# Two transformer layers with dilated window attention and a SiLU feed-forward: the layout of two DRAM scratches, the release of second-layer weight loads, and the planner's landing times

## The chip, the core and the metric

The kernel runs on one core of one Trainium2 chip. Its engines are TensorE (PE in the profile, with weight loads as PEld), VectorE (DVE), ScalarE (ACT), GpSimd (POOL) and SyncE (SP). SP computes nothing here: it issues DMA loads, stores and DMA transposes. The metric is device microseconds of one execution. Before the change the median of three runs is 2185.98 us (2184.86 to 2187.14).

## The reference

One sequence of 2,048 tokens of width 576 goes through attention, feed-forward, attention, feed-forward, each with its own layer norm in front and a residual sum behind. Both layers use the same weights.

```python
H = 32; Dh = D // H          # 18
W, dil = 8, 2
idx = pos[:, None] - off[None, :]          # off = arange(W) * dil
mask = idx >= 0
logits = jnp.einsum("bhsd,bhswd->bhsw", q, kg) * scale
attn = _softmax(jnp.where(mask[None, None, :, :], logits, -1e9), axis=-1)
o = jnp.einsum("bhsw,bhswd->bhsd", attn, vg)          # then @ wo
...
h = _silu(jnp.einsum("bsd,df->bsf", x, w1))           # 576 -> 4608
out = jnp.einsum("bsf,fd->bsd", h, w2)                # 4608 -> 576
...
x = x + _A_ref(_layernorm(x, axis=-1), A_wqkv, A_wo)
x = x + _B_ref(_layernorm(x, axis=-1), B_w1, B_w2)    # both lines twice
```

A token attends to itself and to seven earlier tokens, two positions apart.

## The kernel before

**Stages.** The 2,048 tokens are cut into four chunks of 512 tokens (TB = 4 x 128): two halves of the sequence, and in each the even and the odd positions, so that a window of dilation 2 becomes eight neighbouring rows. Two layers times four chunks give eight stages s = 0 to 7. A stage has a front (load x, attention in four head groups u of 144 columns, projection with wo, layer norm) and a feed-forward. PE works in float16; a float32 value is split in a high and a low half, and a product takes three partial products.

**Feed-forward.** Stages 0 and 1 use plain tiles: 36 column blocks f of w1 (first product, line 1183) and of w2 (second product, line 1202). Stages 2 to 7 use pairs (`ffn_pairs`): two column blocks form a pair q, and each 2x2 block product is made of seven products P1 to P7 instead of eight, with sums of weights ("weight forms", seven 128x640 float16 tiles per pair) against sums of tokens ("token forms"). The seven products of a pair are line 1087, in the order P5, P1, P3, P6, P2, P7, P4. The 18 pairs of a stage are cut into groups of 5, 4, 5 and 4. When a group's hidden tiles stand, `second` (line 1141) multiplies them with the w2 tiles: for each of four token tiles j, and each pair, 12 matmuls.

**Scratches in DRAM.** Split weights go through DRAM: `w1s`, `w2s` (one tensor per block), and `wfs[q]` for the weight forms, which `prepare` makes on DVE, ACT and POOL between stages 0 and 2 and stores from GpSimd (line 1012). `wfs[q]` is 128 rows of 7 x 640 values, so that one form is 128 pieces of 1,280 bytes, 8,960 bytes apart. Keys and values that are computed ahead in stage 0 go to `kd[par][u]`, one row of 288 float32 values (1,152 bytes) per token, stored by SP (line 686); the attention of stages 1 to 3 fetches, for each partition, 11 neighbouring rows as one run of 12,672 bytes (line 713; stage 1 from SP, stages 2 and 3 from GpSimd).

**Buffers.** There are 12 slots for weight forms (`wf`) and 11 for w2 tiles (`w2`). A load takes the next slot, and SP waits until PE has finished with what was there.

**What sets the order.** The instructions aren't issued where they are written. Each `op(engine, duration, function, reads, writes, prio, ...)` goes into a `Plan`. `Plan.order()` plays the whole program through with the given durations, and on each engine starts the ready operation with the lowest `prio` whose slots are free. A transfer is taken to run at `DMA_RATE`, to begin `DMA_IN` after its issue and to be landed `DMA_OUT` after its last byte. The sequence found in this way is then each engine's program. On the chip each engine works through its list in order: an instruction whose semaphore isn't there holds up all that stand behind it on the same engine. So a number in the plan changes no work, but it can change the order on all five engines.

**Names used below.** `load_wf` (line 1015) loads one weight form (160 KB), `load_w2` (856) one w2 tile (288 KB), `load_wq` one qkv weight (1,080 KB), `load_w1` one w1 block. `transposed` (459) turns layer-normed or attention tiles by DMA transpose, `forms` (1062) the token forms. In the trace a `wf` slot bears the name of its memory, `w`; the token forms lie in `xb`; `yh` and `yo` are the tiles that are turned.

## Time and profile before

| | |
|---|---|
| median of 3 runs | 2185.98 us |
| profiled execution, its own time | 2186.47 us |
| its span on the core | 2184.3 us |
| PE busy | 2119.9 us (97%) |
| DVE busy | 1605.7 us (74%) |
| ACT busy | 954.5 us (44%) |
| POOL busy | 364.3 us (17%) |
| granted clock of TensorE, mean | 0.994 |

Between the span and the execution's own time lie 2.2 us. Read the profile like this: first the busy shares, which tell the engine that is short of idle time; then the waits of that engine, each with what ended it; then the time line around the longest of these waits on the engine that waits and on the queue that it waits for. A busy share is a mean over stages with different limits, so what one wait is worth is read where it stands.

### The profile page before, as it was taken

Reading aid. Unit: us, or ns where it says so; the run is one execution under the profiler, and the core shown is the slowest. Engines: PE = TensorE matmul, PEld = TensorE weight load, DVE = VectorE, ACT = ScalarE, POOL = GpSimd, SP = SyncE. Lnnn points to the kernel's source line nnn. Section 1 sums busy time; section 2 is a strip of 40 time slices with the busy share of each in tenths; the row PEclk is TensorE's granted clock in tenths of the full one; section 3 lists DMA queues with packets and bytes.
Section 4 is the critical chain, followed back from the end, with each engine's and each line's share of the span. In section 5 each row is a group of like instructions: output and inputs, shape, how many; then the busy total and the mean of one; then the engine's idle time right before and its main releaser. Section 6 shows DMA issues by size and latency. Waiting matters only on the chain.

```text
span 2184.3 us, 41276 instructions
## 1 busy us (share of the span) xinstructions
PE 2119.9 (97%) x16198; PEld 1578.8 (72%) x16198; DVE 1605.7 (74%) x2539; ACT 954.5 (44%) x1795; POOL 364.3 (17%) x585
## 2 busy tenths in 40 slices
PE   6999999999999899999999999999999999999999
PEld 3546566656666678876788768887787867888887
DVE  7999998999896897548974599646995569852222
ACT  7545687644344453443324434243433424343232
POOL 2133556234333140001100010000000000000000
PEclk9999999999999999999999999999999999999999
DMA  6476777587879785876539666496655855565443
GB/s 178 149 208 240 244 260 250 176 277 268 194 183 314 229 273 176 197 232 187 165 104 254 164 205 179 111 263 156 203 161 148 237 155 149 160 182 176 140 149 108
DMA packets 334234, 426.19 MB, mean 195 GB/s; under 512 B 145608, under 2 KB 262708, under 8 KB 330072
## 3 DMA queue, kind: packets, MB, share of 16 engines
q1 hardware_dynamic: 292464, 289.10, 47.3%
q0 software_dynamic: 38304, 129.28, 18.3%
q10 hardware_dynamic: 3272, 5.19, 0.9%
q8 instruction: 126, 2.06, 0.4%
q14 instruction: 68, 0.56, 0.1%
HBM read 307.32 MB, written 67.68 MB: 172 GB/s over the span
## 4 chain that ended last, share of the span: by engine, by line
PE 81%; DVE 8%; DMA 7%; ACT 2%; issue 1%; POOL 1%; SPq 0%; ACTq 0%; DVEq 0%
PE acc L1141 25%; PE misc L1087 11%; PE z L1087 11%; PE z L670 8%; PE acc L1202 8%; PE z L1183 7%; PE misc L670 5%; PE acc L841 4%; DMA w<-wfs 3%; DVE lg L773 1%; DVE pr L802 1%; DVE pr L769 1%; DVE pr L809 1%; DMA w<-w2s 1%; DMA wq<-in_B_w_dram 1%
## 5 line engine op out<-in xcount | busy, mean ns | idle before, releaser
L1141 PE MATMUL acc<-w,h 128*128 128x288 f16 x5184 | 653.7, 286 | 2.2 <-DVE h L1120 1.6
L1141 PEld LDWEIGHTS <-h 128*128 128x128 f16 x5184 | 506.5, 98 | 130.4 <-DVE h L1120 1.9
L1087 PEld LDWEIGHTS <-w 128*128 128x128 f16 x5292 | 518.9, 98 | 97.3 <-DMA w<-wfs 21.4
L1087 PE MATMUL z<-xb,w 128*128 128x256 f16 x2653 | 339.2, 275 | 14.0 <-DMA w<-wfs 9.9
L1087 PE MATMUL misc<-xb,w 128*128 128x256 f16 x2639 | 333.9, 273 | 10.4 <-DMA w<-wfs 8.6
L848 DVE SCALAR_TENSOR_TENSOR x<-acc,d,x 128x576 f32<-128x576 f32 x135 | 109.5, 812 | 179.1 <-PE acc L1141 171.2
L670 PEld LDWEIGHTS <-xa 128*128 128x128 f16 x1344 | 132.1, 99 | 116.7 <-issue 9.3
L1202 PE MATMUL acc<-w,h 128*128 128x288 f16 x1728 | 214.6, 286 | 0.0
L1202 PEld LDWEIGHTS <-h 128*128 128x128 f16 x1728 | 168.9, 98 | 43.9
L769 DVE TENSOR_TENSOR pr<-qt,kvs 128x2304 f32<-128x2304 f32 x64 | 163.4, 2553 | 34.6 <-DMA kvs<-kvs 24.7
L802 DVE TENSOR_TENSOR pr<-kvs,pe 128x1152 f32<-128x1152 f32 x128 | 169.9, 1352 | 1.1
L773 DVE TENSOR_REDUCE lg<-pr 128x128 f32<-128x2304 f32 x64 | 163.0, 2547 | 1.1
L809 DVE TENSOR_TENSOR pr<-pr 128x1152 f32<-128x1152 f32 (+1 forms) x128 | 135.2, 1056 | 3.4
L1183 PE MATMUL z<-xb,w 128*128 128x512 f16 x588 | 130.8, 383 | 6.0 <-ACT w L918 2.4
L1120 DVE SCALAR_TENSOR_TENSOR h<-wq,sh,h 128x1024 f16<-128x1024 f32 x60 | 76.9, 1281 | 72.6 <-ACT h L1117 72.6
L670 PE MATMUL z<-wq,xa 128*128 128x432 f16 x588 | 114.1, 350 | 4.2 <-ACT w L683 4.2
L841 PE MATMUL acc<-wo,yo 128*128 128x288 f16 x896 | 115.9, 289 | 2.3 <-DMA yo<-yh 2.2
L670 PE MATMUL misc<-wq,xa 128*128 128x432 f16 x588 | 113.1, 349 | 0.8 <-ACT qt L740 0.8
L1183 PEld LDWEIGHTS <-w 128*128 128x128 f16 x588 | 57.5, 98 | 76.6 <-DVE w L920 2.9
L841 PEld LDWEIGHTS <-yo 128*128 128x128 f16 x896 | 88.1, 99 | 27.1 <-DMA yo<-yh 2.7
L750 POOL DMA_DIRECT2D kvs<-kvs x64 | 33.8, 535 | 374.8 <-ACT qt L740 348.1
L1183 PE MATMUL z<-xb,wq 128*128 128x512 f16 x420 | 93.2, 379 | 0.7 <-ACT hs L1185 0.7
(227 smaller groups left out, 2495.5 us busy)
## 6 DMA issues: line engine op xcount, KB each, us to landing
w<-wfs SPq DMA_DIRECT2D x756, 160.0 KB
w<-w2s SPq DMA_DIRECT2D x252, 288.0 KB
wq<-wqs SPq DMA_DIRECT2D x17, 1080.0 KB
kvs<-kd POOLq DMA_DIRECT2D x8, 1584.0 KB, 8.6
w<-w1s SPq DMA_DIRECT2D x36, 320.0 KB
wfs<-xa POOLq DMA_DIRECT2D x18, 640.0 KB, 4.9
w2s<-w POOLq DMA_DIRECT2D x36, 288.0 KB, 4.1
w1s<-wq POOLq DMA_DIRECT2D x30, 320.0 KB, 4.1
```

The lines of the kernel that those rows point to most:

```text
L670: nc.tensor.matmul(T(m)[:, :3 * UC], a, b, start=n == 0, stop=n == len(pl) - 1)
L769: nc.vector.tensor_tensor(T(pr), T(qt)[:, j:j + 2, None, :].to_broadcast([P, 2, W, UC]), win(T(kv), j, 2), op=ALU.mult)
L773: nc.vector.tensor_reduce(T(lg)[:, j:j + 2].rearrange("p a w h -> p (a w h)"), T(pr).rearrange("p a w (h d) -> p (a w h) d", d=DH), axis=A ...
L802: nc.vector.tensor_tensor(T(pr)[:, a].rearrange("p w (h d) -> p w h d", d=DH), v, T(pe)[:, j + a, :, :, None].to_broadcast([P, W, UH, DH]) ...
L809: nc.vector.tensor_tensor(t[:, :, 0:h, :], t[:, :, 0:h, :], t[:, :, h:2 * h, :], op=ALU.add)
L841: nc.tensor.matmul(T(acc)[:, h, 0:288], a, b[:, h * 288:(h + 1) * 288], start=n == 0, stop=n == len(pl) - 1)
L848: nc.vector.scalar_tensor_tensor(t, T(acc)[:, :, 0:288], d, t, op0=ALU.mult, op1=ALU.add)
L1087: nc.tensor.matmul(t, w[:, u, :], v[:, r, :], start=first and m == 0, stop=m == 6, skip_group_check=True)
L1120: op("DVE", 1.2, lambda hq=hq, h=h, sc=sc: nc.vector.scalar_tensor_tensor(T(h)[:, 1].rearrange("p f t -> p (f t)"), T(hq).rearrange("p r t ...
L1141: nc.tensor.matmul(T(acc)[:, h, 0:288], T(hb[t])[:, a, f, j * P:(j + 1) * P], T(wbs[t][f])[:, w, h * 288:(h + 1) * 288], start=t == 0 and ...
L1183: nc.tensor.matmul(T(z), v, u, start=m == 0, stop=m == len(pl) - 1)
L1202: nc.tensor.matmul(T(acc)[:, h, 0:288], T(hb[q])[:, a, j * P:(j + 1) * P], T(wbs[q][0])[:, w, h * 288:(h + 1) * 288], start=q == 0 and m = ...
```

## The change

Five edits:

1. **Key scratch pitch.** A row of `kd` becomes 2 x 144 + 16 = 304 values (1,216 bytes), of which 288 are used. A fetch now reads 11 pieces of 1,152 bytes per partition instead of one run of 12,672 bytes.
2. **Weight forms in blocks.** `wfs[q]` becomes seven blocks of 128 x 640: one form is a contiguous 160 KB. A store from GpSimd writes 4 or 3 pieces of 1,280 bytes per partition instead of one run of 5,120 or 3,840 bytes.
3. **Second weights later.** In a group, the two w2 loads of the third, fourth and fifth pair get one more condition: the product P5 of the pair two before must have been done.
4. **More time in the plan.** An op has a new field `extra`, which is added to the landing time: 3.0 for the DMA transposes of `transposed` at positive priority, 2.0 for those of `forms`, 1.0 for the loads of weight forms. No instruction is added for it.
5. **`product` returns its op**, so that 3 can name it.

```diff
-    def op(self, eng, dur, fn, reads=(), writes=(), prio=0.0, nbytes=0, table=None, after=(), lanes=1):
+    def op(self, eng, dur, fn, reads=(), writes=(), prio=0.0, nbytes=0, table=None, after=(), lanes=1, extra=0.0):
         o = Op()
+        o.extra = extra
...
-                        o.end = clock + self.DMA_OUT
+                        o.end = clock + self.DMA_OUT + o.extra
...
-    wfs = [tc.dram_tile([P, 7 * KB], F16, name=f"wfs{q}") for q in range(NP)]
+    wfs = [tc.dram_tile([7, P, KB], F16, name=f"wfs{q}") for q in range(NP)]
...
+    KP = 2 * UC + 16
...
-    kd = [[tc.dram_tile([W - 1 + 2 * TB, 2 * UC], F32, name=f"kd{p}{u}") for u in range(NU)] for p in range(2)]
+    kd = [[tc.dram_tile([W - 1 + 2 * TB, KP], F32, name=f"kd{p}{u}") for u in range(NU)] for p in range(2)]
...
         return op("SP", 1.34, lambda: nc.sync.dma_start_transpose(dst(), fl(T(src))), [(src, 0), (src, 1)], [(key, j)], prio,
-                  nbytes=P * 9 * P * 4)
+                  nbytes=P * 9 * P * 4, extra=3.0 if prio > 0 else 0.0)
...
-                nc.sync.dma_start(rows(kd[par][u], W - 1 + blk * TB + j, [[NJ * 2 * UC, P], [1, 2 * UC]]),
+                nc.sync.dma_start(rows(kd[par][u], W - 1 + blk * TB + j, [[NJ * KP, P], [1, 2 * UC]]),
                                   stage(g)[:, UC:])
...
-                    q.dma_start(T(kv).rearrange("p a b c -> p (a b c)"),
-                                rows(kd[par][u], row, [[NJ * 2 * UC, P], [1, NI * 2 * UC]]))
+                    q.dma_start(T(kv).rearrange("p a b c -> p a (b c)"),
+                                rows(kd[par][u], row, [[NJ * KP, P], [KP, NI], [1, 2 * UC]]))
...
-    def load_w2(f, prio, kind="w2"):
+    def load_w2(f, prio, kind="w2", after=()):
         w = Buf(kind)
-        op("SP", 0.38, lambda: nc.sync.dma_start(fl(T(w)), w2s[f]), [("w2s", f)], [w], prio, nbytes=P * 4 * D)
+        op("SP", 0.38, lambda: nc.sync.dma_start(fl(T(w)), w2s[f]), [("w2s", f)], [w], prio, nbytes=P * 4 * D, after=after)
...
-                wfs[q][:, r0 * KB:r1 * KB], T(g).rearrange("p i a b -> p (i a b)")), [(g, 0)], [("wfs", q, r0 // 4)], prio, nbytes=P * n * KB * 2)
+                wfs[q][r0:r1].rearrange("i p c -> p i c"), T(g).rearrange("p i a b -> p i (a b)")), [(g, 0)], [("wfs", q, r0 // 4)], prio, nbytes=P * n * KB * 2)
...
-        op("SP", 0.38, lambda: nc.sync.dma_start(fl(T(w)), wfs[q][:, i * KB:(i + 1) * KB]), [("wfs", q, i // 4)], [w], prio, nbytes=P * KB * 2)
+        op("SP", 0.38, lambda: nc.sync.dma_start(fl(T(w)), wfs[q][i]), [("wfs", q, i // 4)], [w], prio, nbytes=P * KB * 2, extra=1.0)
...
                 op("SP", 1.26, lambda f=f, a=a, x=x: nc.sync.dma_start_transpose(T(x)[:, :, a * P:(a + 1) * P], T(f)[:, a]),
-                   [(f, a, 0), (f, a, 1)], [(x, a)], prio, nbytes=P * KB * 4)
+                   [(f, a, 0), (f, a, 1)], [(x, a)], prio, nbytes=P * KB * 4, extra=2.0)
...
-                w2b = [load_w2(2 * q + f, pd) for f in range(2)]
+                w2b = [load_w2(2 * q + f, pd, after=begun[-2:-1] if q > q0 + 1 else ()) for f in range(2)]
...
-                    op("PE", 0.763, mm, [wf[k], (xf[k], 0), (xf[k], 1)], [z], pp)
+                    return op("PE", 0.763, mm, [wf[k], (xf[k], 0), (xf[k], 1)], [z], pp)
...
-                product("P5", c, True, False)
+                begun.append(product("P5", c, True, False))
```

The line numbers of the changed kernel are two or three higher (858 becomes 861, 1017 becomes 1020, 1062 becomes 1065, 1245 becomes 1248). Up to the beginning of stage 1's second half PE's order stays as it is. Behind it the order changes on all engines. Three places of SP's queue:

**SP, the loads for the first group of stage 2**, the first stage in pairs. `wfs1` to `wfs4` are the weight forms of pairs 1 to 4, `w2s2` to `w2s10` the w2 blocks of pairs 1 to 5, two blocks to a pair, `x5` is an x tile of stage 3. Before:

```order
L1245 DMA x5_79<-in_A_x_dram 128x576
L858 DMA w2_93<-w2s2_162 128x1152
L858 DMA w2_93<-w2s3_163 128x1152
L858 DMA w2_93<-w2s4_164 128x1152
L858 DMA w2_93<-w2s5_165 128x1152
L858 DMA w2_93<-w2s6_166 128x1152
L858 DMA w2_93<-w2s7_167 128x1152
L858 DMA w2_93<-w2s8_168 128x1152
L858 DMA w2_93<-w2s9_169 128x1152
L858 DMA w2_93<-w2s10_170 128x1152
L1017 DMA w1_70<-wfs1_197 128x640 x2
L1017 DMA w1_70<-wfs2_198 128x640 x7
```

Now, at the same place:

```order
L861 DMA w2_93<-w2s4_164 128x1152
L861 DMA w2_93<-w2s5_165 128x1152
L1020 DMA w1_70<-wfs1_197 128x640
L1248 DMA x5_79<-in_A_x_dram 128x576
L1020 DMA w1_70<-wfs2_198 128x640 x7
L1020 DMA w1_70<-wfs3_199 128x640 x7
L861 DMA w2_93<-w2s6_166 128x1152
L861 DMA w2_93<-w2s7_167 128x1152
L1020 DMA w1_70<-wfs4_200 128x640 x7
L861 DMA w2_93<-w2s8_168 128x1152
```

Nine w2 loads stood in one block ahead of the rest of the weight forms. Now four stand ahead, among the last forms of pair 1, and the others behind the forms of pairs 3 and 4. In stages 3 to 7 most blocks of this kind are spread in the same way; in stage 2's later groups they still stand together.

**SP, the end of stage 1's loads**, where the token forms of stage 2 are turned; `w1s33` to `w1s35` are the last w1 blocks of stage 1. Before:

```order
L858 DMA w2_93<-w2s35_195 128x1152
L1062 DMA_TRANSPOSE xb_67<-yo_73 128x5x128 x2
L853 DMA w1_70<-w1s33_157 128x1280
L858 DMA w2_93<-w2s0_160 128x1152
L853 DMA w1_70<-w1s34_158 128x1280
L858 DMA w2_93<-w2s1_161 128x1152
L853 DMA w1_70<-w1s35_159 128x1280
```

Now:

```order
L861 DMA w2_93<-w2s35_195 128x1152
L1065 DMA_TRANSPOSE xb_67<-yh_91 128x5x128
L861 DMA w2_93<-w2s0_160 128x1152
L861 DMA w2_93<-w2s1_161 128x1152
L856 DMA w1_70<-w1s33_157 128x1280
L1065 DMA_TRANSPOSE xb_67<-yo_73 128x5x128
L856 DMA w1_70<-w1s34_158 128x1280
L856 DMA w1_70<-w1s35_159 128x1280
```

The two transposes of `yo` stood ahead of all three w1 loads; now the first w1 load is ahead of them, and each of them has moved back. Further ahead in stage 1, SP issues the second pair of `yo<-yh` transposes one w1 load later than before, and PE's projection of stage 2 (line 841) stands one first product (14 matmuls of line 1183) later.

**SP, the token forms of stage 4**, at the end of stage 3's loads. Before:

```order
L1062 DMA_TRANSPOSE xb_67<-yh_91 128x5x128 x2
L1245 DMA x4_78<-xd10_112 128x576
L1245 DMA x5_79<-xd11_113 128x576
L858 DMA w2_93<-w2s3_163 128x1152
L858 DMA w2_93<-w2s4_164 128x1152
L858 DMA w2_93<-w2s5_165 128x1152
```

Now:

```order
L1248 DMA x5_79<-xd11_113 128x576
L861 DMA w2_93<-w2s3_163 128x1152
L1065 DMA_TRANSPOSE xb_67<-yo_73 128x5x128 x2
L1020 DMA w1_70<-wfs1_197 128x640 x2
L861 DMA w2_93<-w2s4_164 128x1152
L1065 DMA_TRANSPOSE xb_67<-yh_91 128x5x128 x2
L1020 DMA w1_70<-wfs2_198 128x640 x2
L861 DMA w2_93<-w2s5_165 128x1152
```

All seven pairs of transposes stood ahead of the w2 block. Now the last three stand among w2 loads and weight forms of the stage's own first pairs, whose slots come free only while PE works on that stage's first products. In stages 6 and 7 two or three pairs have moved in the same way, in stages 3 and 5 only the last pair, behind one w2 load.

More of the change, by code (lines that the diff above doesn't have):

```diff
@@ L56 @@
 class Op:
-    __slots__ = ("eng", "dur", "fn", "prio", "seq", "deps", "outs", "n", "bufs", "nbytes", "start", "end", "table", "lanes")
+    __slots__ = ("eng", "dur", "fn", "prio", "seq", "deps", "outs", "n", "bufs", "nbytes", "start", "end", "table", "lanes", "extra")
 class Plan:
```

7 lines of the change are left out of this document (4 added, 3 removed).

## The prediction

> **What bounds the kernel now.** The page comes first: its span, and the engine with the least idle time.
>
> ```profile
> span 2184.3 us, 41276 instructions
> PE 2119.9 (97%) x16198; PEld 1578.8 (72%) x16198; DVE 1605.7 (74%) x2539; ACT 954.5 (44%) x1795; POOL 364.3 (17%) x585
> ```
>
> PE idles 2184.3 - 2119.9 = 64.4 us. The change takes no matmul away, so it can win no more than a part of this, and what a slowed PE loses behind a wait. The waits of PE, longest first, tell which part (total, times, longest):
>
> ```profile
> PE misc L583 <- DVE nt L482: 13.1, 1, 13.1
> PE z L1087 <- DMA w<-wfs: 9.9, 2, 8.4
> PE misc L1087 <- DMA w<-wfs: 8.6, 6, 2.5
> PE z L670 <- ACT w L683: 4.2, 1, 4.2
> PE acc L841 <- DMA yo<-yh: 2.2, 1, 2.2
> PE acc L1141 <- DVE h L1120: 1.6, 1, 1.6
> PE z L1183 <- DMA w<-w1s: 1.4, 1, 1.4
> ```
>
> The 13.1 us are the program's beginning, in front of everything that moves. Weight forms that come late cost 9.9 + 8.6 = 18.5 us in eight waits, turned tiles 2.2, a w1 load 1.4: 22.1 us wait for DMAs. PE's time line shows where they lie and what comes behind them (start, duration, in brackets the idle time before):
>
> ```profile
> 588.96 8.71 PE L841 MATMUL acc<-wo,yo 128*128 128x288 f16 x56 [2.25 <-DMA yo<-yh]
> 709.85 2.62 PE L1141 MATMUL acc<-w,h 128*128 128x288 f16 x20 [1.64 <-DVE h L1120]
> 720.89 1.68 PE L1087 MATMUL z<-xb,w 128*128 128x256 f16 x7 [8.42 <-DMA w<-wfs]
> 723.08 3.15 PE L1087 MATMUL z<-xb,w 128*128 128x256 f16 x14 [0.51 <-DVE yo L1094]
> 732.36 0.93 PE L1087 MATMUL misc<-xb,w 128*128 128x256 f16 x7
> 1031.66 1.70 PE L1087 MATMUL misc<-xb,w 128*128 128x256 f16 x14 [2.52 <-DMA w<-wfs]
> 1294.28 2.47 PE L1087 MATMUL misc<-xb,w 128*128 128x256 f16 x21 [1.05 <-DMA w<-wfs]
> 1685.09 1.09 PE L1087 MATMUL misc<-xb,w 128*128 128x256 f16 x7 [2.08 <-DMA w<-wfs]
> 1687.47 2.52 PE L1087 MATMUL misc<-xb,w 128*128 128x256 f16 x14
> 1815.44 4.11 PE L1087 MATMUL z<-xb,w 128*128 128x256 f16 x21 [1.50 <-DMA w<-wfs]
> 402.61 3.43 PE acc L841 x28
> ```
>
> (The last row is from the chain of waits.) A wait costs more than its idle time: 7, 14 and 21 matmuls take 0.93, 1.70 and 2.47 us, but 1.68, 3.15 and 4.11 behind some waits. The windows show why:
>
> ```profile
> 700.00:712.00 12.00, 10.36 (x93) 8.79 (x92) 7.91 (x8) 5.26 (x10) 6.41 (x10) 1.00 1.03 349
> 712.00:721.00 9.00, 0.58 (x5) 0.26 (x4) 2.82 (x2) 0.00 (x0) 5.37 (x8) 0.74 1.08 279
> 721.00:724.00 3.00, 2.49 (x12) 1.60 (x12) 1.39 (x2) 0.51 (x1) 0.00 (x0) 0.50 1.07 252
> ```
>
> The three last numbers are the granted clock, the DMA share and GB/s. Behind the wait the clock is 0.50, and the DMA engines are full all through. Extra time behind four of the waits: (1.68 - 0.93) + (3.15 - 1.70) = 2.2 at 720; 8.71 - 2 x 3.43 = 1.85 at 589; at 1815 4.11 - 2.47 = 1.64; at 1685 0.16 in the first row and 0.82 in the 14 matmuls, with a product between them about 1.7. That makes 7.4 us.
>
> **Why the forms come late at 712.** SP's time line:
>
> ```profile
> 660.41 11.63 SPq L1017 DMA_DIRECT2D w<-wfs  x10
> 692.71 9.82 SPq L858 DMA_DIRECT2D w<-w2s  x9
> 705.01 24.86 SPq L1017 DMA_DIRECT2D w<-wfs  x19
> w<-wfs SPq DMA_DIRECT2D x756, 160.0 KB
> w<-w2s SPq DMA_DIRECT2D x252, 288.0 KB
> ```
>
> The 12 slots hold twelve forms, and PE had started twelve products when it stopped. The rest of the forms stands behind nine w2 loads: 9 x 288 KB = 2.6 MB, 7.4 us at the 349 GB/s of the window. They were issued from 692.7 to 702.5; the forms from 705.0 on, into full engines.
>
> **The change, part by part.**
>
> *A, the first group of stage 2.* In the new order four w2 loads (1.2 MB, 3.3 us) stand ahead of pair 2's forms, not nine, and the rest between later forms. Each form load is then held only by its slot, twelve products back, 12 x 0.76 = 9.2 us before it is needed. Also, PE now does 17 products before the first second-layer matmuls where it did 12, so that the hidden tile has four microseconds more and the 1.64 us go too. 8.42 + 1.64 + 2.2 = 12.3; I take -12. The waits that the deferral adds (a w2 load waits for P5 two pairs back) hold up forms behind it on SP, but the first of these forms needs a slot that is freed two products later still; so the condition is met by then.
>
> *B, the ends of stage 1.* At 589 the projection now stands one first product later, 14 matmuls of 128x512, about 3.0 us, more than 2.25: -2.25 - 1.85. At 662 the w1 load moves ahead of two transposes: -1.4. Together -5.5. The two transposes move back past it; they are read from 698 on, over 30 us later.
>
> *C, the seven other waits for forms*: 18.5 - 8.4 = 10.1, and 1.7 + 1.64 of slow clock, 13.4 in all. The w2 blocks ahead of them are spread too. But these waits are short, and some have another cause, a qkv load that stands ahead of the forms, waits for its own slot and holds up SP for ten microseconds:
>
> ```profile
> 1010.31 0.32 SPq L1017 DMA_DIRECT2D w<-wfs  x1
> 1020.53 0.32 SPq L616 DMA_DIRECT2D wq<-wqs  x1
> ```
>
> The qkv loads move too, but stay among the forms. All or nothing are the bounds; I take six tenths, -8.
>
> *D, transposes of token forms moved back* (stages 4, 6 and 7, two or three pairs each; in 3 and 5 the last pair). They now stand behind loads whose slot PE itself frees, nine to eleven products (6.9 to 8.4 us) ahead of the product that reads them. The nearest price is the pair of 576:
>
> ```profile
> 575.89 8.42 SPq L459 DMA_TRANSPOSE yo<-yh  x2
> L1062 SPq DMA_TRANSPOSE xb<-yh x44: 1199/1216/2177, 633.9 to 1964.1; - x44
> ```
>
> Issued by 584.3, read at 588.96: 4.65 us to land when engines are full, and 2 x 1.22 to issue: 7.1 us, as long as the lead. Below: 0. Above: three waits like that at 589, 3 x 4.1 = 12.3. I take a wait of 0.9 us in each of three stages and one slow stretch of clock, 1.7: +4.5.
>
> *E, key rows.* Eleven pieces per partition instead of one. SP's issue price, one piece against three:
>
> ```profile
> L713 SPq DMA_DIRECT2D kvs<-kd x4: 319/320/505, 145.2 to 272.8; - x4
> L573 SPq DMA_DIRECT2D w<-in_A_wqkv_dram x12: 539/612/1088, 13.9 to 22.5; - x12
> 146.26 9.75 DMA kd<-w
> 158.85 14.62 PE L670 MATMUL z<-wq,xa 128*128 128x432 f16 x70 [4.24 <-ACT w L683]
> ```
>
> 0.15 us a piece makes +1.5 us a fetch. It is on the path once: the store at 146.26, issued behind the fetch of 145.2, frees the staging tile for which PE waits 4.24 us. Above +1.5; below, if the wider pitch made the store quick, -4.24 and 1.7 of clock. The row is nearest to a loss: +1. On GpSimd the eight fetches are not on PE's path.
>
> *Here the Trainium skill, "DMA: Bandwidth & Descriptors", section "Latency and other measured facts", says that a DRAM row pitch at large powers of two halves the rate, that 4 KiB of padding restored it and 192 B did not. The store's pitch goes from 4,608 to 4,864 B; by this rule it gains nothing, and E is +1.5 where the gain would make it -5.9. No row here shows a rate by pitch.*
>
> *F, weight forms in blocks.* A read has the same 128 pieces of 1,280 bytes. A store has four times as many pieces:
>
> ```profile
> L1012 POOL DMA_DIRECT2D wfs<-xa x36: 537/570/800, 465.4 to 829.9; - x36
> L877 POOL DMA_DIRECT2D w<-in_B_w_dram x36 | 27.4, 762 | 10.2 <-DMA qd<-w 8.0 <-issue 2.0
> ```
>
> Line 877 has four pieces and takes 0.76 us against 0.57: 36 x 0.2 = 7 us on an engine that is 17% busy, with the first store at 465 and its first read at 660. I take 0. With that cover gone it would be 0.2 us a store. A faster read could only help C.
>
> *G, the rest of the order.* The small waits of PE for ACT and DVE behind 700 us (0.3 to 0.8 each) sum to some 6 us. They fall elsewhere in a new order: between -3 and +4, I take +1.
>
> Sum: -12 - 5.5 - 8 + 4.5 + 1 + 0 + 1 = -19. The profiled execution took 2186.5 us (2.2 around its span), 0.5 above the median: 2186.0 - 19 = **2167 us**. With A, B and C whole and D, E, G at 0: -31, 2155. With A -10, B -4, C -4, D +8, E +1.5, G +2: -6.5, 2179. That is the forecast's own range.
>
> **Rivals.**
>
> *Given back to DVE: 2177.* Behind 730 DVE has no room, and PE's products need its sums:
>
> ```profile
> 740.00:750.00 10.00, 10.00 (x88) 8.38 (x87) 9.86 (x12) 3.46 (x7) 0.00 (x0) 1.00 0.56 169
> DVE yo L1094 <- PE z L1087: 7.8, 1, 7.8
> ```
>
> If DVE's work up to 860 sets when PE can go on to stage 3, A is worth only its clock, 2.2 instead of 12, and the sum is -9. Against it speaks the second row: DVE itself stood 7.8 us in the same wait, behind a sum for a product that hadn't come. It gets this time back as well.
>
> *The forms now starve in every group: 2196.* This is the slower case. While products run, a pair takes 7 x 0.76 = 5.3 us and asks for 7 x 160 + 2 x 288 = 1,696 KB, 317 GB/s, close to the 349 of the full window. Before, the w2 tiles came partly while second-layer matmuls ran, when nothing else was asked for; now they come with the forms, and SP's order puts them ahead. There are 24 groups. If one in three waits like the 1815 one, 1.50 + 1.64 = 3.1 us, that is +25, against A and B (-17.5) and +2 for E and G: +10. It decides from six groups on. Against it: the form loads still have their twelve products of lead.
>
> *The plan's numbers do nothing: 2186.* The waits at the old places go and as much comes back at new ones (D at its upper bound, C at nothing, A half).
>
> **How the numbers follow.** Forecast 0.60, given back 0.16, nothing 0.09, starved 0.15. About 0.2% (4.4 us) is what a measurement of this kernel can tell from no change. Forecast and the DVE case are faster by more, less a little at their upper edges: 0.75; same 0.10; slower 0.15. The range goes from 2155 to 2187: it holds the forecast, the DVE case and the case of nothing, and leaves out the starved case and a little below.
>
> **What would show it.** A: no wait over 2 us for `wfs` between 700 and 730, and no granted clock of 0.50 there. B: no wait for `yo<-yh` near 589, none for `w1s` near 661. C: the waits for `wfs` sum to 4 to 6 us instead of 18.5. D: new waits of PE for `xb<-yh` or `xb<-yo` at the beginnings of stages 4, 6 and 7, some 1 us each. E: the wait at 154.6 is 4 to 6 us. F: line 1012 near 0.76 us, PE's order untouched. I am wrong if PE's idle time isn't some 12 us smaller, or if it is and the span isn't; a sum of `wfs` waits over 25 us means the starved case, and new waits for DVE between 730 and 860 the first rival.

## The result, and the profile after

The change makes the kernel slightly slower, not 19 us faster. In twelve runs of each it takes 2189.45 us (2186.98 to 2191.99) against 2184.62 us (2178.79 to 2187.20), a ratio of 1.0027 with a 95% interval of 1.0018 to 1.0036. The page of the changed kernel:

```profile
span 2189.9 us, 41155 instructions
PE 2118.1 (97%) x16198; PEld 1580.0 (72%) x16198; DVE 1600.8 (73%) x2539; ACT 963.3 (44%) x1801; POOL 377.7 (17%) x585
```

The span grew by 5.6 us. PE is idle for 71.8 us, where it was 64.4 (+7.4), and busy for 1.8 us less; its mean granted clock was 0.996, where it was 0.994. Who ended its waits (total, times, longest; the main rows):

```profile
PE z L1090 <- DMA w<-wfs: 8.0, 3, 3.2
PE misc L1090 <- DVE hs L1097: 4.1, 2, 3.4
PE misc L1090 <- DMA w<-wfs: 2.7, 3, 1.3
PE misc L1090 <- DVE wq L1097: 2.7, 4, 0.9
PE z L1090 <- DMA xb<-yo: 1.5, 1, 1.5
PE acc L844 <- DMA yo<-yh: 1.2, 1, 1.2
PE z L1186 <- DMA w<-w1s: 1.1, 1, 1.1
PE z L1186 <- ACT h L1190: 2.3, 1, 2.3
```

The waits for DMAs fell as intended, from 22.1 to 8.0 + 2.7 + 1.5 + 1.2 + 1.1 = 14.5 us. Over all rows of the view (the program's start left out), the waits for DVE rose from 9.6 to 19.0 and those for ACT from 15.5 to 21.7 us. So 7.6 us were won at DMAs and 15.6 lost at the engines that empty PE's banks and make its inputs.

Where along the program this happened is best read by stage. A stage ends here with its last second-layer matmul on PE's time line; the table has the time between two such ends in us, and, for stages 4 to 6, how long before (-) or after (+) the stage's first product SP issued the last transpose of its token forms.

| kernel | 1 | 2 | 3 | 4 | 5 | 6 | 7 | last transpose, 4 / 5 / 6 |
|---|---|---|---|---|---|---|---|---|
| before | 231.2 | 233.7 | 261.2 | 261.1 | 261.9 | 261.5 | 202.9 | -10.2 / -9.6 / -12.1 |
| after | 231.4 | 233.5 | 259.4 | 264.1 | 264.4 | 262.2 | 203.8 | +12.8 / -2.3 / +21.2 |
| e2 (edit 3) | 231.1 | 228.9 | 262.4 | 261.7 | 261.5 | 260.6 | 202.9 | -8.9 / -7.6 / -10.9 |
| e7 (edit 3, loads' 1.0) | 232.1 | 228.6 | 257.1 | 257.1 | 257.7 | 259.5 | 202.9 | -4.5 / -4.9 / -4.3 |
| e10 (after, no forms' 2.0) | 227.2 | 231.0 | 257.3 | 260.3 | 264.9 | 260.7 | 202.1 | -2.7 / +15.2 / +15.5 |
| e14 (after, no turned 3.0) | 228.9 | 231.4 | 257.9 | 258.2 | 259.3 | 259.2 | 202.9 | -2.8 / -3.0 / -2.8 |
| e15 (after, no loads' 1.0) | 230.4 | 238.7 | 259.6 | 259.7 | 263.2 | 269.7 | 202.9 | -2.0 / +8.2 / +14.0 |
| e17 (e7, late transposes) | 227.9 | 232.8 | 267.7 | 267.6 | 269.4 | 270.1 | 209.2 | +12.1 / +12.7 / +12.2 |
| e19 (edit 3, loads' 2.0) | 229.7 | 226.2 | 258.7 | 258.6 | 257.9 | 258.6 | 202.9 | -1.1 / -1.4 / -1.9 |

Each row is one profiled execution. How far a cell can stray shows in e4 and e8 (below), whose order is on every engine that of the changed kernel: they took 231.5 and 226.5 us in stage 1, 228.8 and 238.2 in stage 2, and differ from it by up to 3 us in a later stage. So a single cell of stage 2 says little, and one of the later stages nothing below some 3 us. What stands out: in the changed kernel stage 2, which was to win 12 us, is as long as before, and stages 4 to 7 are 7.1 us longer in sum (5.7 in e4, 3.5 in e8).

**Stage 2.** PE's time line of the changed kernel, and its windows (PE, PEld, DVE, ACT, POOL busy, then clock, DMA share, GB/s):

```profile
709.32 1.65 PE L1090 MATMUL misc<-xb,w 128*128 128x256 f16 x7 [3.43 <-DVE hs L1097]
719.32 1.67 PE L1090 MATMUL z<-xb,w 128*128 128x256 f16 x7 [2.81 <-DMA w<-wfs]
```

```profile
706.00:709.00 3.00, 0.00 (x0) 0.00 (x0) 2.96 (x3) 0.00 (x0) 0.57 (x1) 0.80 1.03 401
709.00:712.00 3.00, 2.68 (x13) 1.87 (x13) 3.00 (x4) 1.50 (x3) 0.73 (x1) 0.50 1.02 369
712.00:715.00 3.00, 3.00 (x17) 2.08 (x15) 1.34 (x3) 1.62 (x2) 1.46 (x2) 0.56 1.03 332
715.00:718.00 3.00, 1.04 (x9) 0.58 (x6) 3.00 (x4) 1.08 (x3) 1.45 (x2) 1.00 0.67 194
718.00:721.00 3.00, 1.68 (x8) 1.19 (x9) 1.73 (x3) 0.42 (x2) 2.81 (x4) 0.51 0.54 124
721.00:724.00 3.00, 3.00 (x16) 2.12 (x15) 0.00 (x0) 1.82 (x3) 2.95 (x5) 0.50 1.00 265
724.00:727.00 3.00, 3.00 (x24) 2.39 (x23) 2.04 (x3) 2.15 (x4) 0.70 (x1) 0.85 1.01 274
```

The wait of 8.42 us has become two of 3.43 and 2.81, each with a stretch of clock 0.50 that begins in it. The DMA engines are full up to 715 us (1.02 to 1.03) and again from 721; in between, while PE waits for the second time, their share is 0.67 and 0.54. The first of the two waits has a new cause, on DVE:

```profile
703.79 2.56 DVE L772 TENSOR_TENSOR pr<-qt,kvs 128x2304 f32<-128x2304 f32 x1 [3.79 <-DMA qt<-qd]
706.38 2.55 DVE L776 TENSOR_REDUCE lg<-pr 128x128 f32<-128x2304 f32 x1
708.85 0.41 DVE L1097 TENSOR_TENSOR hs<-misc,hs 128x256 f32<-128x256 f32 x1
```

In the new order the logits of stage 3 stand ahead of the sums that empty PE's banks. They wait for the fetch of query and key rows, and PE waits behind them.

The second wait is for a weight form. What SP waited for before it could issue form loads, from 704 to 722 us of the changed kernel:

```profile
SPq L1020 <- DMA w<-wfs: 5.3, 5, 1.7
SPq L1020 <- DMA w<-w2s: 4.2, 3, 2.0
SPq L1020 <- PE misc L1090: 0.2, 1, 0.2
```

It waited 9.5 us for earlier weight loads to land (and 1.9 for an x load) and 0.2 us for PE to free a slot. In the trace SP's transfers use eight landing semaphores in turn, and a transfer that uses one again goes out only when the transfer eight issues before it has landed: the form load of 708.99 went out when that of 699.94 had landed, at 708.93. The form load that ended PE's wait was issued at 705.22 and landed at 719.28, 14.1 us later. In the kernel before the same waits for landings of weight loads are there, 12.6 + 1.2 us in this window, and none for a slot.

**The start of stage 4.** PE first (the stage's projection in two rows, its first product, the waits behind), then SP:

```profile
1138.62 7.02 PE L844 MATMUL acc<-wo,yo 128*128 128x288 f16 x56
1152.36 7.02 PE L844 MATMUL acc<-wo,yo 128*128 128x288 f16 x56
1191.90 0.93 PE L1090 MATMUL z<-xb,w 128*128 128x256 f16 x7
1196.64 0.94 PE L1090 MATMUL z<-xb,w 128*128 128x256 f16 x7 [1.52 <-DMA xb<-yo]
1203.41 0.94 PE L1090 MATMUL z<-xb,w 128*128 128x256 f16 x7 [2.02 <-DMA w<-wfs]
1208.75 1.70 PE L1090 MATMUL misc<-xb,w 128*128 128x256 f16 x14 [1.35 <-DMA w<-wfs]
```

```profile
1172.92 2.53 SPq L1065 DMA_TRANSPOSE xb<-yo  x2
...
1196.04 2.56 SPq L1065 DMA_TRANSPOSE xb<-yh  x2
1198.69 1.00 SPq L1020 DMA_DIRECT2D w<-wfs  x2
...
1203.39 2.52 SPq L1065 DMA_TRANSPOSE xb<-yo  x2
1206.01 5.29 SPq L1020 DMA_DIRECT2D w<-wfs  x11
```

The projection for stage 4 ends at 1159.4, 32 us before the first product of that stage; before it was 58 us (1131.80 + 3.60 = 1135.4 against 1193.4, the last row of the next view). So the token forms are made later, and SP still turns them while PE runs the first products. A transpose that is late makes PE wait once for itself (1.52) and then for the form loads that stand right behind a pair of transposes on SP (2.02 for one issued at 1198.69, 1.35 for one issued at 1206.01). The kernel before:

```profile
1131.80 3.60 PE L841 MATMUL acc<-wo,yo 128*128 128x288 f16 x28
1193.38 0.93 PE L1087 MATMUL z<-xb,w 128*128 128x256 f16 x7
```

### The profile page after: what moved, and what is told of

It reads as the page before. It is cut to its first block, busy times and chain, and to the rows that moved or that the text cites. A ratio compares the mean times of both kernels' runs of the same rounds, so it can differ in the third digit from the quotient of the medians.

```text
span 2189.9 us, 41155 instructions
## 1 busy us (share of the span) xinstructions
PE 2118.1 (97%) x16198; PEld 1580.0 (72%) x16198; DVE 1600.8 (73%) x2539; ACT 963.3 (44%) x1801; POOL 377.7 (17%) x585
## 4 chain that ended last, share of the span: by engine, by line
PE 74%; DVE 11%; DMA 8%; ACT 3%; issue 2%; POOL 1%; SPq 0%; ACTq 0%; DVEq 0%; POOLq 0%
PE acc L1144 26%; PE misc L1090 11%; PE z L1090 11%; PE acc L1205 7%; PE z L1186 6%; PE z L673 5%; PE acc L844 5%; PE misc L673 4%; DVE pr L805 2%; DMA w<-wfs 2%; DVE pr L812 2%; DVE pr L772 1%; DMA xb<-yo 1%; DVE lg L776 1%; DMA xb<-yh 1%
## 5 line engine op out<-in xcount | busy, mean ns | idle before, releaser
L673 PE MATMUL z<-wq,xa 128*128 128x432 f16 x630 | 119.4, 346 | 2.4 <-ACT w L686 2.4
L1123 DVE SCALAR_TENSOR_TENSOR h<-wq,sh,h 128x1024 f16<-128x1024 f32 x60 | 76.8, 1280 | 51.6 <-ACT h L1120 51.6
L673 PE MATMUL misc<-wq,xa 128*128 128x432 f16 x546 | 106.4, 351 | 0.8 <-ACT qt L743 0.8
L1094 ACT ACTIVATE wq<-z 128x256 f32<-128x256 f32 x93 | 34.9, 376 | 144.4 <-PE z L1090 144.2
## 6 DMA issues: line engine op xcount, KB each, us to landing
kvs<-kd POOLq DMA_DIRECT2D x8, 1584.0 KB, 10.5
```

The costliest lines, as they stand in the source:

```text
L673: nc.tensor.matmul(T(m)[:, :3 * UC], a, b, start=n == 0, stop=n == len(pl) - 1)
L1123: op("DVE", 1.2, lambda hq=hq, h=h, sc=sc: nc.vector.scalar_tensor_tensor(T(h)[:, 1].rearrange("p f t -> p (f t)"), T(hq).rearrange("p r t ...
```

## The experiments

All ratios are to the kernel before, timed on the same chip between the other runs. L stands for the two layouts (edits 1 and 2), D for the deferral (3), and T, F, W for the three landing times of edit 4: turned tiles 3.0, token forms 2.0, loads of weight forms 1.0. The layouts leave every engine's order as it is, so a kernel with them and one without compare layouts alone. The kernel before had medians of 2183.5 to 2185.0 us beside the four groups of runs, so medians of different groups compare to some 1.5 us.

| label | edits | median us | ratio, 95% interval |
|---|---|---|---|
| changed kernel | L D T F W | 2189.45 | 1.0027 (1.0018 to 1.0036) |
| e1_layout | L | 2184.76 | 1.0004 (0.9993 to 1.0014) |
| e2_defer | D | 2181.29 | 0.9990 (0.9979 to 1.0000) |
| e3_landing | T F W | 2201.39 | 1.0072 (1.0051 to 1.0092) |
| e4_order | D T F W | 2188.22 | 1.0020 (1.0004 to 1.0037) |
| e5_defer_turned | D T | 2168.63 | 0.9930 (0.9918 to 0.9942) |
| e6_defer_forms | D F | 2189.41 | 1.0026 (1.0015 to 1.0037) |
| e7_defer_loads | D W | 2166.82 | 0.9923 (0.9911 to 0.9935) |
| e8_oldpitch | L (forms only) D T F W | 2191.69 | 1.0033 (1.0021 to 1.0045) |
| e10_after_no_forms | L D T W | 2175.26 | 0.9958 (0.9940 to 0.9976) |
| e14_after_no_turned | L D F W | 2171.57 | 0.9942 (0.9925 to 0.9958) |
| e15_after_no_loads | L D T F | 2197.72 | 1.0060 (1.0040 to 1.0080) |
| e11_loads | W | 2181.72 | 0.9988 (0.9975 to 1.0000) |
| e16_loads_layout | L D W | 2167.63 | 0.9922 (0.9908 to 0.9936) |
| e17_loads_late | D W, transposes held back | 2224.16 | 1.0179 (1.0162 to 1.0196) |
| e18_after_forms1 | L D T W, F at 1.0 | 2184.18 | 0.9998 (0.9987 to 1.0009) |
| e19_loads2 | D, W at 2.0 | 2166.57 | 0.9913 (0.9900 to 0.9926) |

**First four: which edit.** The layouts alone (e1) and the deferral alone (e2) in the kernel before; the core of each:

```diff
-    wfs = [tc.dram_tile([P, 7 * KB], F16, name=f"wfs{q}") for q in range(NP)]
+    wfs = [tc.dram_tile([7, P, KB], F16, name=f"wfs{q}") for q in range(NP)]
...
-    kd = [[tc.dram_tile([W - 1 + 2 * TB, 2 * UC], F32, name=f"kd{p}{u}") for u in range(NU)] for p in range(2)]
+    kd = [[tc.dram_tile([W - 1 + 2 * TB, KP], F32, name=f"kd{p}{u}") for u in range(NU)] for p in range(2)]
```

> The kernel before with the two layouts alone (key rows at a pitch of 304 floats, weight forms in blocks); on every engine the order stays that of before. Theory 1 (the key fetches in 11 pieces land later: 21.2 us at most behind the change, 13.1 before, and DVE and with it PE stand behind one of them): slower by 3 to 6 us, some fetch of stage 3's rows lands after more than 15 us, line 1012's counterpart takes 0.76 us and the fetch's issue on GpSimd 1.1 us. Theory 2 (the new order is the cause, layouts are neutral): within 1.5 us of before.

```diff
-                w2b = [load_w2(2 * q + f, pd) for f in range(2)]
+                w2b = [load_w2(2 * q + f, pd, after=begun[-2:-1] if q > q0 + 1 else ()) for f in range(2)]
```

> The kernel before with the condition on the second weights alone. My prediction's step A put 12 us on the first group of stage 2; if that is owed to the deferral, the wait of 8.4 us for a weight form goes and the run is 5 to 12 us faster. Theory 2 (what the deferral wins at DMA waits comes back as waits of PE for DVE and ACT): 0 to 5 us slower, waits for weight forms under 12 us, waits for DVE and ACT (sums and snaps of the products) 8 us more than before. Theory 1: faster by 3 us or more, since no layout is changed.

The three landing times alone (e3), and together with the deferral (e4), which is the changed kernel without its layouts:

```diff
-                  nbytes=P * 9 * P * 4)
+                  nbytes=P * 9 * P * 4, extra=3.0 if prio > 0 else 0.0)
...
-        op("SP", 0.38, lambda: nc.sync.dma_start(fl(T(w)), wfs[q][:, i * KB:(i + 1) * KB]), [("wfs", q, i // 4)], [w], prio, nbytes=P * KB * 2)
+        op("SP", 0.38, lambda: nc.sync.dma_start(fl(T(w)), wfs[q][:, i * KB:(i + 1) * KB]), [("wfs", q, i // 4)], [w], prio, nbytes=P * KB * 2, extra=1.0)
...
-                   [(f, a, 0), (f, a, 1)], [(x, a)], prio, nbytes=P * KB * 4)
+                   [(f, a, 0), (f, a, 1)], [(x, a)], prio, nbytes=P * KB * 4, extra=2.0)
```

> The kernel before with the longer landing times in the plan alone. Theory 1: not slower than before. Theory 2: slower by 1 to 5 us, with new waits for ACT or DVE. Rival 3 (any change of the plan's numbers draws another order by chance): a result between -5 and +5 us with waits at places that have nothing to do with turned tiles or form loads.

> The changed kernel without the two layouts: on every engine the order of the changed kernel, but key rows fetched as one run and forms in the old scratch. Theory 1: DVE's wait of 3.8 us for the query rows at 703.8 goes, the fetch lands within 15 us, PE's 3.4 us behind it and the slow clock behind that go too; 4 to 8 us below the changed kernel, so equal to or faster than before. Theory 2: no less than the changed kernel less 1.5 us, still slower than before.

Measured: the layouts cost about 1 us, inside the interval of no change, and taking them out of the changed kernel wins 1.2 us of its 4.8. Theory 1 falls. The deferral alone wins 2.3 us, at the edge of what can be told; step A and theory 1 asked for more, theory 2 for a loss. The landing times alone cost 16 to 18 us (by the ratio and by the medians), where theory 2 had 1 to 5; in e4 theory 2 is right. So edit 4 carries the loss, and the deferral hides most of it. That the deferral doesn't win step A's 12 us shows in e2's own rows, PE's wait and the window around it:

```profile
715.01 1.67 PE L1088 MATMUL z<-xb,w 128*128 128x256 f16 x7 [5.98 <-DMA w<-wfs]
```

```profile
710.00:720.00 10.00, 4.99 (x27) 3.58 (x28) 4.51 (x2) 1.53 (x4) 6.47 (x9) 0.66 1.08 270
```

With only four w2 loads ahead of the forms, PE still waits 5.98 us, and the DMA engines are full (1.08). The load that ended this wait was issued at 702.05 and took 12.9 us to land.

**Second four: which number.** e5, e6 and e7 are the deferral with one line each of the diff of e3: turned tiles, token forms, form loads.

> The deferral and the 3.0 us for turned tiles alone, no layouts. The deferral alone gave 2181.3 us, with all three landing times 2188.2. If one number carries the 7 us and it is this one: 2186 to 2190 here, and 2180 to 2183 in the two kernels with the others. If each number draws another order and all of them cost a part: 2183 to 2186 in each of the three.

> The deferral and the 2.0 us for the transposes of token forms alone. My step D: these transposes come later on SP in stages 4, 6 and 7. If they carry the loss: 2186 to 2190 here, with stages 4 to 7 some 1 to 3 us longer each than with the deferral alone. If not: 2180 to 2183.

> The deferral and the 1.0 us for weight-form loads alone. The plan then sees every product of the pairs later, so its orders on PE, DVE and ACT move most. If this carries the loss: 2186 to 2190, with new waits of PE for the sums and snaps of its products (DVE, ACT). If not: 2180 to 2183; below 2180 it would be of use.

e8 takes the pitch back in the changed kernel, with its stores and fetches:

```diff
-    kd = [[tc.dram_tile([W - 1 + 2 * TB, KP], F32, name=f"kd{p}{u}") for u in range(NU)] for p in range(2)]
+    kd = [[tc.dram_tile([W - 1 + 2 * TB, 2 * UC], F32, name=f"kd{p}{u}") for u in range(NU)] for p in range(2)]
```

> The changed kernel with the old pitch of the key rows (fetches in one run), forms in blocks kept; the order is the changed one. Stage 2 took 233.5 us in the changed kernel's profile and 228.8 in the one without both layouts. If the key fetch in 11 pieces makes that: stage 2 takes 228 to 230 us here, no wait of DVE for query rows before 710, and the time is 2 to 5 us below the changed kernel. If the blocks of forms make it: as the changed kernel.

Measured: T wins 13 and W 14 us on top of the deferral, which no theory had asked of them; F loses 8, so that e6 ends in its upper range; but it loses the time at another place than expected, 6.2 us in stage 2 (235.1 against e2's 228.9) and 2.7 in stages 4 to 7. The old pitch wins nothing (2191.69 against 2189.45), and its profile has stage 2 at 238.2 us, where the key fetch as the cause asked for 228 to 230.

**Third four: one number left out at a time, and W without the deferral.** e10, e14 and e15 take one of the three numbers out of the changed kernel; here e14's:

```diff
-                  nbytes=P * 9 * P * 4, extra=3.0 if prio > 0 else 0.0)
+                  nbytes=P * 9 * P * 4)
```

> The changed kernel without the 2.0 us for the transposes of token forms. Theory F (this number carries the loss, as with the deferral alone): 2165 to 2172. Theory L (late token path: what decides is how long before the first product of a stage the projection has ended; in the changed kernel 24 to 46 us in stages 4 to 7 against 57 to 58 before and 49 in the kernel with deferral and loads): the order here puts 24 to 46 us between them as well, so 2178 to 2190, with stages 4 to 6 longer than 260 us.

> The changed kernel without the 3.0 us for turned tiles; layouts, deferral, forms' 2.0 and loads' 1.0 kept. Theory F: 2185 to 2192, since the forms' number is still there. Theory L: in this order the projection ends 49 us of PE's work ahead of the first product in each of stages 4 to 7, so 2164 to 2173, with stages 4 to 6 at 257 to 260 us and token-form transposes issued before the first product.

> The changed kernel without the 1.0 us for form loads. Theory F: 2185 to 2192. Theory L: leads of 46, 37, 30 and 49 us in stages 4 to 7, between the good and the bad orders: 2176 to 2188, stage 6 the longest.

e11 is the kernel before with the 1.0 of the form loads:

```diff
-        op("SP", 0.38, lambda: nc.sync.dma_start(fl(T(w)), wfs[q][:, i * KB:(i + 1) * KB]), [("wfs", q, i // 4)], [w], prio, nbytes=P * KB * 2)
+        op("SP", 0.38, lambda: nc.sync.dma_start(fl(T(w)), wfs[q][:, i * KB:(i + 1) * KB]), [("wfs", q, i // 4)], [w], prio, nbytes=P * KB * 2, extra=1.0)
```

> The kernel before with the 1.0 us for form loads alone, no deferral. With the deferral it gave 2166.8 us, the deferral alone 2181.3. If the number alone does it: 2165 to 2172. If it takes both (the number moves the products, the deferral takes the second weights out of their way): 2178 to 2186. Theory L alone (lead 58 us, as before): as before, 2181 to 2186.

Measured: without F the changed kernel is 14 us faster, without T 18 us faster, without W 8 us slower. Theory F misses all three: e10 is 3 us above its range, e15 6 above, and e14, with F still there, 13 below. Theory L is right for e14, 3 us too high for e10 and 10 us too low for e15. W alone gives 1.8 us, with the deferral 17 (against the kernel before): it takes both. T is neither good nor bad by itself: it wins 13 us on the deferral, loses 8 next to W (e10 against e16, below), 8 next to F (e15 against e6, the layouts' 1 us in it) and 18 next to both. F always loses: 8 us on D, 4 with W (e14 against e16), 29 with T (e15 against e5, with the layouts' 1 us), 14 with both. F and W add up to within 4 us (8 and -14 alone, -10 together); T and W don't (-13 and -14 alone, -6 together).

In e7 the token forms are turned earlier than in the changed kernel and end in time (the last projection, the first and the last transposes, the first product):

```profile
1134.30 3.59 PE L843 MATMUL acc<-wo,yo 128*128 128x288 f16 x28
1187.05 0.93 PE L1089 MATMUL z<-xb,w 128*128 128x256 f16 x7
```

```profile
1151.16 1.21 SPq L1064 DMA_TRANSPOSE xb<-yo  x1
...
1181.21 2.52 SPq L1064 DMA_TRANSPOSE xb<-yo  x2
```

**Last four: the layouts in a good order, lateness by itself, and doses.** e16 is e7 with edits 1 and 2.

> The deferral and the 1.0 us for form loads with both layouts: the changed kernel without the landing times of turned tiles and token forms. Without the layouts this order gave 2166.8 us. If the layouts cost nothing on PE's path: 2165 to 2169. If the key fetches in 11 pieces or the stores in blocks cost what stage 2's profiles seem to show (3 to 5 us): 2170 to 2173.

e17 is e7 with the transposes of token forms held until a second-layer step of the stage before (`seconds` collects these steps); stage 3's are held in the same way.

```diff
-                    op("PE", 0.737 * len(hs_), mm2, [(hb[t], 0), (hb[t], 1)] + wbs[t], [(acc, h) for h in hs_], pp)
+                    seconds.append(op("PE", 0.737 * len(hs_), mm2, [(hb[t], 0), (hb[t], 1)] + wbs[t], [(acc, h) for h in hs_], pp))
...
-                   [(f, a, 0), (f, a, 1)], [(x, a)], prio, nbytes=P * KB * 4)
+                   [(f, a, 0), (f, a, 1)], [(x, a)], prio, nbytes=P * KB * 4, after=seconds[-13:-12])
```

> The 2166.8 us kernel (deferral, loads' 1.0), with one more condition: the DMA transposes of token forms of stages 4 to 7 wait for the fourth of the last sixteen second-layer steps of the stage before, so that they start some 19 us ahead of the first product, as in the changed kernel's stage 4, and not 36 us. No landing time is changed. Theory L (late token forms are what costs): stages 4 to 6 each 3 to 8 us longer than 257 to 259 us, in all 2178 to 2192. If their lateness is harmless and the loss lies in something else that the orders have in common: 2166 to 2171.

e18 puts 1.0 for 2.0 in the changed kernel's line of the token forms, e19 puts 2.0 for 1.0 in e7's line of the form loads.

```diff
-                   [(f, a, 0), (f, a, 1)], [(x, a)], prio, nbytes=P * KB * 4, extra=2.0)
+                   [(f, a, 0), (f, a, 1)], [(x, a)], prio, nbytes=P * KB * 4, extra=1.0)
```

> The changed kernel with 1.0 instead of 2.0 us for the transposes of token forms; with none it took 2175.3 us, with 2.0 2189.5. Theory L (a longer planned path makes the token forms later by degrees): 2178 to 2186. If each number just draws another order: anything from 2166 to 2200, and no relation to the two neighbours.

```diff
-        op("SP", 0.38, lambda: nc.sync.dma_start(fl(T(w)), wfs[q][:, i * KB:(i + 1) * KB]), [("wfs", q, i // 4)], [w], prio, nbytes=P * KB * 2, extra=1.0)
+        op("SP", 0.38, lambda: nc.sync.dma_start(fl(T(w)), wfs[q][:, i * KB:(i + 1) * KB]), [("wfs", q, i // 4)], [w], prio, nbytes=P * KB * 2, extra=2.0)
```

> The 2166.8 us kernel with 2.0 instead of 1.0 us for form loads. In its order the projection ends 45 us of PE's work ahead of the first product of stages 4 to 7 (49 with 1.0, 46 in the 2168.6 us kernel). Theory L: 2164 to 2171. If 1.0 was a lucky draw: above 2175.

Measured: the layouts cost 0.8 us in the good order, nothing that can be told. F by dose: 2175.3, 2184.2, 2189.5 us at 0, 1.0 and 2.0, and e18 is where theory L had it. But three values in rising order come out by chance one time in six, and the way that theory L gives isn't seen: stages 4 to 6 sum to 785.9, 780.9 and 790.7 us in these three profiles, and the leads of the projection don't fall by degrees either. So that F works through late token forms is not shown. W at 2.0 is as good as at 1.0. e17 is 57 us slower than e7, far more than expected; its transposes run from 20 us before to 12 us after the first product, as in stage 4 of the changed kernel, and each of the stages 3 to 6 is 10.5 to 11.7 us longer than in e7. What PE waits for there:

```profile
PE misc L1090 <- DMA xb<-yo: 13.9, 3, 5.5
PE z L1090 <- DMA xb<-yh: 4.7, 2, 4.4
PE misc L1090 <- DMA xb<-yh: 4.1, 1, 4.1
```

So holding the token forms back can cost what the changed kernel lost, and more. Two things keep this from being its cause: in e17 PE waits for the tiles themselves (22.7 us in these rows), in the changed kernel 1.5 us; and the condition is part of the plan, so other work moves in e17 too.

Over stages 4 to 6 of all these profiles but e17's (51 stages): where the last transpose was issued 1 to 6 us ahead of the first product, a stage took 259.5 us in the mean (21 stages, 257.1 to 264.4); 6 to 12 us ahead 261.2 (15, 259.5 to 262.9); after it 263.6 (15, 259.5 to 269.7). The groups overlap, and the kernels in them differ in more than this. In stage 3 of the same profiles the relation isn't there: issued after the first product (6 stages, 4 to 13 us) 258.7 us in the mean, ahead of it (11) 259.6. The shortest stage of all is e18's stage 3, 256.4 us, with its last transpose 12.9 us after the first product and no wait of PE for it; in e17's stage 3, at 13.3 us, PE waits 5.9 us for two such tiles. So a late transpose costs by where the products that read it stand in PE's order, and the time of its issue alone doesn't tell.

The fastest kernel, with e7 and e16 too close to tell apart, is e19, the deferral with 2.0 us for form loads, no layouts and nothing for T and F: 18 us under the kernel before, 23 under the changed one. Its page, and the longer row of its waits for forms (the other has 0.5 us):

```profile
span 2162.0 us, 41152 instructions
PE 2112.7 (98%) x16198; PEld 1578.3 (73%) x16198; DVE 1601.6 (74%) x2539; ACT 961.4 (44%) x1803; POOL 365.6 (17%) x585
```

```profile
PE z L1089 <- DMA w<-wfs: 3.2, 2, 2.8
```

PE idles 49.3 us, 15.1 less than before, and there the waits for DMAs sum to 7.7 us while those for DVE (8.9) and ACT (17.1) stay about where they were. That is the size of the gain that I had forecast, but not for its reasons: stage 2 gave 7.5 us, stages 3 to 6 11.9 and stage 1 1.5. That the sizes agree is luck.

## Why the prediction was wrong

The sum was -19 us; measured were +4.8 us by the medians and +5.6 by the spans. By the spans the sum missed by 24.6 us: 11.8 of them lie in step A, 5.7 in B and 7.8 in stages 3 to 7, for which C, D and G were nearly all meant (-2.5 forecast, +5.3 measured); outside stages 1 to 7 the span grew by 0.3, where E had +1. Step A is the step that failed first and the largest error.

**A failed, -12 against -0.2 (stage 2, 233.7 to 233.5).** The step that failed is "each form load is then held only by its slot". Between 704 and 722 us slots held them for 0.2 us, and landings of earlier weight loads for 9.5: SP issues a transfer only when the one eight issues before it has landed. The rest of the forms went out earlier, from 699.9 and not from 705.0, but into DMA engines that were full up to 715, and the load that PE waited for took 14.1 us to land. I had quoted the full engines (1.08), and the waits of SP for landings stood in the profile before; I drew no consequence from either. That the full engines make the landings slow is argued from the shares; no run takes the other transfers away, and from 715 to 721 the share was down to 0.67 and 0.54 while SP still waited for landings. The deferral alone is worth 4.8 us there in e2's profile, and a wait of 5.98 stays. In the changed kernel the sign that I had named is broken twice: a wait over 2 us for `wfs` (2.81), and two stretches of clock 0.50 where there was one. Over the profiles stage 2 takes 228.7 us in the mean in the six kernels with the deferral and without F (e17 left out; 226.2 to 231.0), 234.3 in the three with neither (233.7 to 234.9), and again 234.3 in the six with the deferral and F at 2.0 (228.8 to 238.7). So the deferral is worth some 5.6 us there, half of what I put, and F, of which the step took no account, gives as much back. How F does this is not shown: in the changed kernel's profile it is the wait for DVE at 709, but with the same order e4 has no such wait, and e6 loses the time at another place, in a wait of 5.99 us for a form at 787.

**B, -5.5 against +0.2 (stage 1).** The stage has two halves of the projection. Before the first, the 3.0 us of work that I put ahead of it were enough: its wait of 2.25 us and the slow clock behind it are gone. What I left out is the second half, whose transposes SP now issues behind one more w1 load; it waits where it had not:

```profile
590.01 7.02 PE L844 MATMUL acc<-wo,yo 128*128 128x288 f16 x56
604.30 7.03 PE L844 MATMUL acc<-wo,yo 128*128 128x288 f16 x56 [1.22 <-DMA yo<-yh]
```

The wait for `w1s` went from 1.4 to 1.1 us, and waits for ACT (2.3 for `h` at 665, 0.7 at 660) came in addition. With the same order e4's stage 1 took as long (231.5) and e8's 226.5, so a part of B may be lost by chance in this profile.

**C, -8.** The waits for forms sum to 10.7 us, where I asked for 4 to 6; before they were 18.5. Of this fall of 7.8 us, 5.6 lie at the one place of step A (8.42 to 2.81), so the rest hardly fell. A new one, in the middle of stage 5 on PE's time line (its load stood behind a qkv load and two w2 loads and took 10.3 us to land):

```profile
1546.56 0.94 PE L1090 MATMUL z<-xb,w 128*128 128x256 f16 x7 [3.19 <-DMA w<-wfs]
```

**D was right in its place in stage 4, and too small.** I priced a late transpose with the tile that PE waits for, 0.9 us in each of the stages 4, 6 and 7. Stage 4 shows one such wait, 1.52. What I left out is what the transposes hold up behind them on SP (2.02 + 1.35 for forms), and that the projection, from which they start, moves back by 12 to 37 us against the first product (leads of 32, 46, 24 and 36 us in stages 4 to 7; 57 to 61 before). Stages 4 to 7 took 7.1 us more than before, of which stage 4's three waits make 4.9; stages 5 to 7 show no wait for token forms, and how much of their part is due to them is open. Against e7 stages 4 to 7 took 17 us more: in a good order they become shorter than before.

**E: the wrong price and the wrong cover.** SP's issue price for a fetch and GpSimd's, in the changed kernel:

```profile
L716 SPq DMA_DIRECT2D kvs<-kd x4: 371/371/580, 146.9 to 271.5; - x4
L716 POOL DMA_DIRECT2D kvs<-kd x8: 1079/1113/1136, 322.0 to 753.6; - x8
```

The same line on GpSimd in the kernel before (shortest, median and longest in ns):

```profile
L713 POOL DMA_DIRECT2D kvs<-kd x8: 533/538/549, 323.1 to 757.9; - x8
```

The wait of PE's time line at the place of 154.6 us:

```profile
159.56 10.75 PE L673 MATMUL z<-wq,xa 128*128 128x432 f16 x58 [2.39 <-ACT w L686]
```

On SP eleven pieces cost 0.05 us more than one, not 1.5: my price of 0.15 us a piece came from float32 weight loads of three pieces and didn't carry over. The wait that I expected at 4 to 6 us is 2.39; over the profiles it is 2.3 to 3.0 us with the wide pitch (7) and 2.9 to 4.2 without (11), a gain of some 0.7 us. The Trainium skill ("DMA: Bandwidth & Descriptors", "Latency and other measured facts") gives rates for row pitches of 512 KiB and more; at 4 MiB the rate is halved and a padding of 192 B does not restore it. The pitch here is 4,608 B, and no run shows a rate by pitch. And "on GpSimd the eight fetches are not on PE's path" is wrong in this order: the issue doubled from 0.54 to 1.11 us, the median fetch landed after 10.5 us instead of 8.6, the longest after 21.2, and DVE and then PE stood behind it at 703.8 (the key rows had landed at 702.7, the query rows, issued right behind them, at 703.7). With the same order and the old single run, DVE went through without a wait for the rows (e4's time line):

```profile
698.55 2.55 DVE L771 TENSOR_TENSOR pr<-qt,kvs 128x2304 f32<-128x2304 f32 x1
```

By the medians this is worth no more than the 1 us of all layouts.

**F right.** One block store takes 0.78 us, and PE's path doesn't see it:

```profile
L1015 POOL DMA_DIRECT2D wfs<-xa x36: 744/782/922, 465.9 to 826.8; - x36
```

**G, +1, was far too small.** I bounded it at +4 as waits behind 700 us that "fall elsewhere in a new order". The waits for DVE and ACT grew by 15.6 us over the program, 3.43 of it in the wait at 709.

**The rivals.** Given back to DVE came nearest: the new waits are for DVE and ACT. But they don't lie where it put them: between 730 and 860 they are 0.77, 0.66 and 0.24 us, no more than before (0.81, 0.47 and 0.71), and its sum (2177) still had B and C in it. Starving didn't come: the form waits fell. (Its 317 GB/s, and the 7.4 us for nine w2 loads, count a KB of the trace as 1,000 bytes; with 1,024 they are 325 GB/s and 7.6 us, which changes no term.) That the plan's numbers do nothing (2186) is the nearest in time, by luck: added to the deferral or left out, each of them moves the time by 4 to 29 us, and A gave nothing where this case still had half of it.

**Open.** Shown is which numbers lose together; the way from the order to the time is traced for single waits in stages 2 and 4 of the changed kernel alone. Why T, good on D, turns bad beside F or W was not traced further than the order: next to both the projection ends 24 to 46 us before the first product of stages 4 to 7, and alone 44 to 48. The waits in the middle of stages 5 and 6 of the changed kernel (3.19 at 1546; 1.10, 1.83 and 0.77 for DVE and ACT between 1804 and 1812) aren't explained by late token forms.

## What to carry to other kernels

A landing time in a list scheduler is no local safety margin: every number moves the whole order, numbers that win alone can lose together, so time each alone and each left out before they go in as a bundle. When loads come late, look first at what holds the queue that issues them: here it was the landing of earlier loads, not the free slot, and with the DMA engines full taking five of nine loads out of the way won 5.6 us of a hoped-for 12. For work that feeds the next stage, look at the first products of each stage on the time line: a late link can cost not only its own wait but that of the loads queued behind it, as in stage 4, or nothing at all, as in e18's stage 3, where PE's order had other products to go on with.

## What was not expected of the hardware

A slow clock needs no long stop. The pause of PE of 3.43 us at 709 came with a half clock from 707.8 to 714.6 us (the windows' 0.80, 0.50 and 0.56 mean 1.2 + 3.0 + 2.6 us of it), the pause of 2.81 with another to 724.9 (0.85). A wait cut in two thus got two slow stretches. Nor does the length decide: in the kernel before the pause of 1.50 us at 1815 came with half a clock, the one of 2.52 at 1031 with none. And the cost of pieces depends on who issues them: eleven instead of one added 0.05 us on SP and 0.57 us on GpSimd.
